# V loaded head by head, folds in halves, end scores apart: one stretch of an attention and MoE kernel

## The chip, the core and the metric

The kernel runs on one core of one Trainium2 chip. The metric is the device time of one execution in microseconds (us); the number for a kernel is the median of its runs. The engines are TensorE (PE; PEld is its weight load), VectorE (DVE), ScalarE (ACT), GpSimd (POOL) and SyncE (SP). DMAs are issued by POOL, which also converts float32 to bfloat16 on the way, by SP, and at the start by ACT.

## The reference, cut

```python
# q, k, v: (8 batches, 8 heads, 576 positions, 64), float32
scores = q @ k.transpose(0, 1, 3, 2) / 8
mask = (rel >= 0) & (rel < 64)          # rel = query position - key position
attn = softmax(where(mask, scores, -1e9))
x = (attn @ v).transpose(0, 2, 1, 3).reshape(4608, 512)
h = x @ w_in                            # 512 -> 2048
out = (h * clip(h + 3, 0, 6) / 6) @ w_out   # 2048 -> 512
```

Causal attention with a window of 64 positions feeds a two-layer network with a hard-swish between the layers.

## The kernel before

The work has two halves that are woven into each other. The network runs over nine tiles of 512 tokens: for tile t the first products (`s1_part`, L737) give 16 blocks of hidden units, each finished by one ACT and one DVE instruction (L750, L755), and the second products (`s2_part`, L776) give four blocks of 128 output rows, 16 matmuls each, which are copied (L789) and stored by SP. Attention of batch t + 1 is placed inside tile t.

Attention of a batch works on pairs of heads, 0 to 3 (`NG` = 4). For batches 0 and 1, q and k arrive with nine positions per partition (tiles `Aq`, `Ak`) and PE turns them ("folds") into `Fq` and `Fk`. In batch 1 `fold_four` (L540) does that for two pairs at once: 36 transposes for q and 36 for k into two PSUM tiles of two banks each, then one copy of 128x1152 per tile (L545), q on ACT and k on DVE here. From batch 2 on, q and k arrive by rows (`nq`, `nk`) and SP issues two DMA transposes into `Tq` and `Tk` (L391), each after the loads that it reads.

`scores` (L581) multiplies q by k for a group of items in one PE piece: an item is a pair, or "e", the last 64 queries of all pairs. Each item has a PSUM tile of its own, an exponential on ACT (L597) and a masking on DVE (L606). In batch 1 the groups are (0, 1) and ("e", 2, 3). `pv_rows` (L626) multiplies by V for a pair, DVE normalises (L636, L637), `turn_x` (L652) transposes the result into `xT` (copy at L368); "e" goes through `pv` (L678, ACT L684 and L687, DVE L698).

V lies in one tile, `V`, by blocks of 128 positions and by pairs. Four blocks are loaded; seven more, each half a block further on, are made by copies between partition halves (`shift_v`, L456), four blocks and three blocks in separate copies. In batch 1 there is a shift for each pair, which the planner gives to POOL, ACT or DVE. Batch 1's V comes by `load_vrows` (L389): four loads with 128 positions of all eight heads each, and a fifth, `load_vrows(1, NE)` for the end rows. Batch 0 has also used `load_vhead`, one load with all four blocks of one head.

What stands where is decided before the program is written. Each operation is put down with its reads and writes, an estimate of its duration, a stream and a priority, and `Plan.solve` places one after the other on the engine and the PSUM tile that let it start first. PSUM has three kinds of tile: "n" (`pn`, two of one bank), "b" (`pb`, one of two banks) and "a" (`pa`, two of two banks). Landing times of DMAs are fixed by hand for the first loads: `LANDED` and, for the loads on POOL after them, the list `NEXT`. POOL's loads and its `hold` operations form one chain through `then`, in the order in which they are put down; its other work is placed between them. The result is one fixed order for each engine. `hold` (L854) is a small POOL copy that keeps the next batch's loads behind a DMA transpose.

Of the kernel before, what the change touches and what calls it, by code (L numbers as in the profile page):

```python
# [11 lines left out]
BF16 = mybir.dt.bfloat16  # L12
# [12 lines left out]
    "POOL": (4600, 6820, 7920, 9640, 10900, 11600, 11950, 12350, 12800, 13200),  # L25
    "ACT": (3200,),
}
NEXT = (15140, 16470, 19010, 21590, 24580, 26640, 29180, 30650, 32050, 32490, 35020, 37600, 39010, 40440, 41280, 42170, 43000, 43830, 44270, 45500, 46500, 47500, 48500, 49500, 50500, 51500, 52500, 53300, 54000)
MARGIN = 300
COLD_PE = 6500  # L30
FAR = 8.0e9
# [191 lines left out]
def kernel(  # L223
# [9 lines left out]
    nc = tc.nc  # L233
    P = nc.NUM_PARTITIONS
    B, H, S, D = q.shape
# [33 lines left out]
    def bank(op, name):  # L269
        s, k = op.got[name]  # L270
        return banks[k][s][:] if k == "n" else banks[k][s][:, 0, :]
# [15 lines left out]
    def t_key(n, b, g):  # L287
        return ("T" if b >= ROWS_FROM else "F") + n, g

    def home(b, g, h):  # L290
        return 1 - h if 0 < b < ROWS_FROM and g % 2 else h
# [61 lines left out]
    def act(n):  # L353
        return 160 + n / 1.2

    def dve(n, fast=1):
        return 150 + n / 0.96 / fast
# [4 lines left out]
    def cpy(eng):  # L362
        return {"DVE": nc.vector.tensor_copy, "ACT": nc.scalar.copy, "POOL": nc.gpsimd.tensor_copy}[eng]
# [9 lines left out]
    def pe(dur, em, reads, writes, stream, alloc=None, kinds=("n",), after=(), mode="f"):  # L373
        op = add("PE", dur, em, reads=reads, writes=writes, stream=stream, after=after)
        op.alloc, op.kinds, op.mode = alloc, kinds, mode
        return op
# [61 lines left out]
    def load_vhead(b, g, h, after=()):  # L438
        return dma(NE * P, 16, V[:, 0:NE, g, 2 * h * D : 2 * h * D + D], v[b, 2 * g + h, 0:MAIN, :].rearrange("(k s) d -> s k d", k=NE),
                   writes=[("V", g, 0, blk) for blk in (2 * h, 2 * h + 1)], eng="POOL", after=after)  # L440
# [85 lines left out]
    def fold_four(g0, b, gate, kinds=("b", "a")):  # L526
# [24 lines left out]
            e.frees = (x,)  # L551
        return op

    def scores(b, items, gate, stream="att", pr=300, masked=False, kinds=("a",)):

        names = tuple(("S", b, x) for x in items)
        keys = [("ps", n) for n in names]
        ends = [x == "e" for x in items]
        gs = sorted({g for x in items for g in (range(NG) if x == "e" else (x,))})
        if masked:  # L560
            add_far = pe(2 * mm(MAIN) + 50, None, ["far", "ident"], keys, stream, alloc=names, kinds=kinds, after=gate)

            def far_em():
                for h in range(2):
                    nc.tensor.matmul(wide(add_far, names[0])[:, h, :], lhsT=ident[:], rhs=far[:].rearrange("p j c -> p (j c)"),
                                     start=True, stop=False)

            add_far.emit = far_em
        op = pe(sum(2 * (NG if e else NM) * 14 for e in ends) + (100 if masked else 0), None,
                [t_key(n, b, g) for g in gs for n in "qk"], keys,  # L570
                stream, alloc=None if masked else names, kinds=kinds, after=gate, mode="r")

        def em():
            for x, name in zip(items, names):
                to = wide(add_far if masked else op, name)
                for y in range(NG if x == "e" else NM):
                    g, j = (y, NM) if x == "e" else (x, y)
                    for h in range(2):
                        r = slice(home(b, g, h) * D, (home(b, g, h) + 1) * D)
                        for o, w in k_cols(b, r, g, j):  # L580
                            nc.tensor.matmul(to[o, home(b, g, h) if x == "e" else h, y * D : (y + 1) * D], lhsT=w,  # L581
                                             rhs=q_cols(b, r, g, j), start=not masked,
                                             stop=not masked or y == NM - 1)

        op.emit = em
        got = []
        for x, name, key in zip(items, names, keys):
            if x == "e":
                n, w, p_, m0 = NG, ("p9", b % 2), p9[b % 2], 1
            else:  # L590
                i = npt[0] % NPT
                npt[0] += 1
                n, w, p_, m0 = NM, ("pT", i), pT[i], 0
                got.append(i)

            def ex(name=name, n=n, p_=p_):
                nc.scalar.activation(out=p_[:].rearrange("p j h c -> p h j c"),  # L597
                                     in_=wide(add_far if masked else op, name)[:, :, 0 : n * D].rearrange("p h (j c) -> p h j c", c=D),
                                     func=EXP, scale=scale)

            e = add("ACT", act(n * P), ex, reads=[key], writes=[w], prio=pr)
            e.frees = (name,)
            if not masked:
                def mk(n=n, p_=p_, m0=m0):
                    pp = p_[:].rearrange("p j h c -> p (j h c)")
                    nc.vector.tensor_tensor(out=pp, in0=pp, in1=mask[:, m0 : m0 + n, :, :].rearrange("p j h c -> p (j h c)"), op=MULT)  # L606

                add("DVE", dve(n * P, 2), mk, reads=["mask"], writes=[w], port=True, prio=pr + 100)
        return op, got
# [184 lines left out]

    def attend(b, first, second, stream="att", rows=()):
        a, i0 = scores(b, (0, 1), first, stream)
        z, i1 = scores(b, ("e", 2, 3), second + (a,), stream, kinds=("b", "a"))
        todo = list(zip((0, 1, "e", 2, 3), (*i0, None, *i1)))
        if rows:
            todo.append(todo.pop(2))  # L800
        for x, i in todo:
            if x in rows:
                _, *og = pv_rows(b, x, i, (z,), stream)
                turn_x(b, x, *og, stream, kinds=("b", "a"))
            else:
                pv(b, x, i, (z,), stream)
# [16 lines left out]
    def load_v(b, blks):  # L823
        for blk in blks:
            then(load_vrows(b, blk, chain))
# [20 lines left out]
    def then(op):  # L846
        chain[0] = op
        return op
# [62 lines left out]
        then(add("POOL", pool(NG * P), lambda n=n: nc.gpsimd.memset(by_block(n, N_)[D:P, KB - 1, :, :], 0.0),  # L911
             writes=[("n" + n, NE, 0), ("n" + n, NE, 1)], after=chain))
    then(add("POOL", 1900, lambda: nc.gpsimd.memset(V[:, :, :, D + 2 : 2 * D], 1.0), writes=["V2"], after=chain))
    load_v(1, range(NE))

    for t in range(NTT):
        head = HEAD if len(x_parts(t)[1]) == 1 else 0
        if t == 0:
            head = HEAD0
            for gs, n in ((range(2), head), (range(2, NG - 1), SOON)):  # L920
                for fc in range(n):
                    s1_part(t, fc, gs)
        else:
            for fc in range(head):
                s1_part(t, fc, range(NG - 1))

        def seen(t, fc, head):
            return 0 if fc >= head else 2 if t == 0 and fc >= SOON else NG - 1

        hs = [s1_finish(t, fc, s1_part(t, fc, range(seen(t, fc, head), NG))) for fc in range(NFC)]  # L930
        ys = {}
        us = range(4 * t, 4 * t + 4)
        if t == 0:
            for pair in (us[:2], us[2:]):
                for part in (range(0, NFC // 2), range(NFC // 2, 3 * NFC // 4), range(3 * NFC // 4, NFC)):
                    for u in pair:
                        ys[u] = s2_part(u, part)
                for u in pair:
                    s2_close(u, ys[u][-1])
        else:  # L940
            for u in us:
                for cols in (((0, DM),) if u < NT // P - 1 else ((0, 3 * P), (3 * P, DM))):
                    s2_close(u, s2_part(u, range(NFC), cols=cols)[-1], cols)
        b = t + 1
        if b < B:
            if b == 1:
                gate = (hs[4],)
                cast_v(iv, 0, 2, (THREE,) * 3, parts=REST, prio=-2500, pieces=(1,))
                scores(0, ("e",), gate, "pick", kinds=("b", "a"))
                pv(0, "e", None, (), "pick")  # L950
                then(load_vrows(1, NE, chain))
                for g in range(0, NG, 2):
                    fold_four(g, 1, gate)
                for g in range(NG):
                    shift_v(g, g + 1, THREE)
                attend(1, gate, gate, "pick", ROWS)
            else:
                for g in range(0, NG, 2):
                    shift_v(g, g + 2, ("ACT", "DVE") if b == 2 else ("DVE",))
                attend(b, (hs[LATE if b > ROWS_FROM else -1],), (hs[-1],))  # L960
            if b + 1 < B:
                load_rows(b + 1)
# [53 lines left out]
```

## Time and profile before

| | us |
|---|---|
| median of 3 runs | 300.29 (299.33 to 302.04) |
| the profiled execution | 299.94 |
| its span, first to last instruction | 298.2 |
| PE busy in the span | 287.2 (96%) |
| ACT busy | 206.5 (69%) |
| DVE busy | 199.8 (67%) |
| POOL busy | 121.9 (41%) |
| mean granted TensorE clock | 0.999 |

Times in the profile are us from the first instruction. A row of the instructions in order of time has the start, the length, the engine, the line, the operation, what it writes and reads, how many there are, and in brackets how long the engine sat idle before and what ended that. In DMA rows the last number is the median time from issue to landing in us. Matmuls are pipelined, so the length of one row reaches into the next one's start. Busy shares are averages over stages with different limits.

### The profile page before, as it was taken

The numbers are of one execution on the slowest core, as the hardware profiler recorded it, in microseconds if no ns is written. First come the engines' busy times: TensorE is split into PE (matmuls) and PEld (weight loads), VectorE is DVE, ScalarE is ACT, GpSimd is POOL, SyncE is SP. The second block draws the span as 40 slices with busy tenths as digits, with TensorE's granted clock in tenths as the row PEclk, the third lists the DMA queues.
The fourth block names the chain that finished last, engine by engine and source line by source line (L and its number), as shares of the span: only waits on it lengthen the run. The fifth ranks groups of instructions, "written<-read, shape, count | busy, mean of one in ns | idle before, by whom it ended". The sixth has DMA issues, their size and how long they took to land.

```text
span 298.2 us, 6926 instructions
## 1 busy us (share of the span) xinstructions
PE 287.2 (96%) x2780; PEld 153.4 (51%) x2825; DVE 199.8 (67%) x327; ACT 206.5 (69%) x319; POOL 121.9 (41%) x170
## 2 busy tenths in 40 slices
PE   6899998999999999999999999999999999999996
PEld 6544555445544554455687554455445544444443
DVE  4768639777777975878678767878677868106700
ACT  3878636887968795778687958886787768227611
POOL 8884667069547916930992069405000000000000
PEclk9999999999999999999999999999999999999999
DMA  8999999999999999989996899969900110110011
GB/s 187 189 207 206 203 191 176 191 95 151 132 201 150 117 151 196 169 55 209 142 165 40 139 184 171 68 118 167 116 2 35 37 70 1 37 70 35 0 73 70
DMA packets 137680, 36.66 MB, mean 123 GB/s; under 512 B 126256, under 2 KB 132912, under 8 KB 137648
## 3 DMA queue, kind: packets, MB, share of 16 engines
q0 software_dynamic: 98816, 17.80, 73.9%
q1 hardware_dynamic: 38688, 18.12, 25.2%
q8 instruction: 22, 0.36, 0.5%
q10 hardware_dynamic: 144, 0.29, 0.4%
q14 instruction: 10, 0.08, 0.1%
HBM read 36.70 MB, written 9.44 MB: 155 GB/s over the span
## 4 chain that ended last, share of the span: by engine, by line
PE 81%; DMA 10%; POOL 3%; issue 3%; DVE 2%; ACT 0%; POOLq 0%; DVEq 0%
PE pn L776 36%; PE pn L737 16%; PE pa L737 12%; PE pb L737 9%; DMA Aq<-in_q_dram 4%; DMA V<-in_v_dram 4%; PE pa L678 4%; DMA Ak<-in_k_dram 2%; PE pa L581 2%; PE pa L776 1%; PE pb L678 1%; DVE opg L637 1%; DVE pT L606 1%; POOL V L389 0%; POOL Aq L389 0%
## 5 line engine op out<-in xcount | busy, mean ns | idle before, releaser
L776 PE MATMUL pn<-wout,gT 128*128 128x512 bf16 x533 | 124.9, 379 | 2.1 <-issue 1.1
L737 PEld LDWEIGHTS <-win 128*128 128x128 bf16 x640 | 62.0, 98 | 60.5
L776 PEld LDWEIGHTS <-gT 128*128 128x128 bf16 x592 | 54.5, 98 | 58.0 <-issue 0.2
L737 PE MATMUL pn<-xT,win 128*128 128x512 bf16 (+1 forms) x270 | 61.1, 357 | 0.3
L750 ACT ACTIVATE t<-pn,half 128x512 bf16<-128x512 f32 x62 | 42.6, 689 | 8.7 <-PE pn L737 8.3
L755 DVE SCALAR_TENSOR_TENSOR gT<-t,pa 128x512 bf16<-128x512 bf16 x47 | 32.2, 687 | 24.2 <-ACT t L750 23.9
L737 PE MATMUL pa<-xT,win 128*128 128x512 bf16 (+1 forms) x202 | 48.0, 358 | 0.4
L755 DVE SCALAR_TENSOR_TENSOR gT<-t,pn 128x512 bf16<-128x512 bf16 x62 | 42.5, 686 | 8.4 <-ACT t L750 8.1
L389 POOL DMA_DIRECT2D nk<-in_k_dram x55 | 42.0, 797 | 4.8 <-DMA Tk<-nk 4.1
L389 POOL DMA_DIRECT2D V<-in_v_dram x40 | 33.2, 848 | 14.4 <-PE pa L678 12.0
L750 ACT ACTIVATE t<-pa,half 128x512 bf16<-128x512 f32 x47 | 32.2, 686 | 8.9 <-PE pa L737 8.5
L698 DVE TENSOR_TENSOR xT<-pa,rec 64x512 bf16<-64x512 f32 (+1 forms) x48 | 32.0, 667 | 9.3 <-ACT rec L687 8.4
L737 PE MATMUL pb<-xT,win 128*128 128x512 bf16 (+1 forms) x153 | 36.3, 357 | 0.5 <-issue 0.5
L755 DVE SCALAR_TENSOR_TENSOR gT<-t,pb 128x512 bf16<-128x512 bf16 x35 | 24.0, 686 | 16.2 <-ACT t L750 16.1
L789 ACT COPY osb<-pn 128x512 f32<-128x512 f32 x18 | 10.5, 585 | 33.1 <-PE pn L776 33.1
L684 ACT ACTIVATE rec<-pa 64x512 f32<-64x512 f32 (+1 forms) x48 | 27.6, 574 | 5.1 <-PE pa L678 4.0
L750 ACT ACTIVATE t<-pb,half 128x512 bf16<-128x512 f32 x35 | 24.2, 690 | 7.6 <-PE pb L737 7.5
L389 POOL DMA_DIRECT2D nq<-in_q_dram x30 | 27.0, 900 | 3.2 <-DMA wout<-in_moe_w_out_dram 1.6
L597 ACT ACTIVATE pT<-pa 128x1024 bf16<-128x1024 f32 x25 | 24.6, 1021 | 1.0 <-PE pa L581 0.9
L606 DVE TENSOR_TENSOR pT<-pT,mask 128x1024 bf16<-128x1024 bf16 x28 | 19.2, 704 | 3.7 <-ACT pT L597 3.6
L678 PEld LDWEIGHTS <-V 128*128 128x128 bf16 x448 | 16.8, 98 | 6.7 <-DVE xT L698 0.8
L854 POOL COPY scrap<-Tq 128x1 bf16<-128x1 bf16 x5 | 0.9, 189 | 45.3 <-DMA Tq<-nq 45.3
(93 smaller groups left out, 203.9 us busy)
## 6 DMA issues: line engine op xcount, KB each, us to landing
out_dram<-osb SPq DMA_DIRECT2D x35, 256.0 KB, 3.1
V<-in_v_dram POOLq DMA_DIRECT2D x28, 128.0 KB, 5.7
nq<-in_q_dram POOLq DMA_DIRECT2D x24, 128.0 KB, 4.7
nk<-in_k_dram POOLq DMA_DIRECT2D x41, 64.0 KB, 4.0
wout<-in_moe_w_out_dram POOLq DMA_DIRECT2D x4, 512.0 KB, 14.5
win<-in_moe_w_in_dram POOLq DMA_DIRECT2D x3, 512.0 KB, 9.3
V<-in_v_dram POOLq DMA_DIRECT2D x12, 64.0 KB, 6.0
Aq<-in_q_dram POOLq DMA_DIRECT2D x2, 288.0 KB, 13.7
```

The source lines that it names most:

```text
L389: em = lambda: e.dma_start(out=out_ap, in_=in_ap)
L581: nc.tensor.matmul(to[o, home(b, g, h) if x == "e" else h, y * D : (y + 1) * D], lhsT=w, rhs=q_cols(b, r, g, j), start=not masked, stop=no ...
L597: nc.scalar.activation(out=p_[:].rearrange("p j h c -> p h j c"), in_=wide(add_far if masked else op, name)[:, :, 0 : n * D].rearrange("p ...
L606: nc.vector.tensor_tensor(out=pp, in0=pp, in1=mask[:, m0 : m0 + n, :, :].rearrange("p j h c -> p (j h c)"), op=MULT)
L678: nc.tensor.matmul(wide(op, name)[:, h, y * D : (y + 1) * D], lhsT=V[:, blk, g, h * D : h * D + P], rhs=p_[:, y, home(b, g, h) if end else ...
L684: add("ACT", act(n), lambda h=h: nc.scalar.activation(out=rc[rows[h], 0:n], in_=wide(op, name)[rows[1 - h], h, 0:n], func=LN), reads=[key] ...
L698: nc.vector.tensor_tensor(out=o, in0=a, in1=z, op=MULT)
L737: nc.tensor.matmul(bank(op, name)[:, to : to + n], lhsT=win16[:, g, fc * P : (fc + 1) * P], rhs=xT[:, g, o : o + n], start=(g == 0), stop= ...
L750: nc.scalar.activation(out=t1[ti][:], in_=bank(op, name), func=RELU, bias=half[:], scale=1.0 / 6.0)
L755: nc.vector.scalar_tensor_tensor(out=gT[:, fc, :], in0=t1[ti][:], scalar=1.0, in1=bank(op, name), op0=MIN, op1=MULT)
L776: nc.tensor.matmul(bank(op, name)[:, 0:n], lhsT=gT[:, fc, col : col + P], rhs=wout16[:, fc, js], start=(fc == 0), stop=(fc == NFC - 1))
L789: alts = {e: (f(n), (lambda e=e: cpy(e)(out=osb[oi][:, js], in_=bank(op, name)[:, 0:n])), False) for e, f in (("DVE", dve), ("ACT", act))}
```

## The change

Batch 1's V is loaded head by head: eight loads of 64 KB in the place of four of 128 KB, and the fifth load of the end rows as before. Pairs 2 and 3 of batch 1 are folded by a new function, first q and then k as two operations, each with two PSUM tiles of which one bank is used, and with one copy of 128x576 for each pair. Pairs 0 and 1 stay with `fold_four`. In batch 1 the scores of "e" become a group of their own, put down after (2, 3). In `NEXT` four fixed landing times are replaced by eight between the same neighbours.

```diff
-NEXT = (15140, ..., 39010, 40440, 41280, 42170, 43000, 43830, 44270, 45500, ...)
+NEXT = (15140, ..., 39010, 40440, 40863, 41287, 41711, 42135, 42558, 42982, 43406, 43830, 44270, 45500, ...)
...
+    def fold_two(n, g0, b, gate, kinds=("b", "a")):
+
+        pair = (g0, g0 + 1)
+        names = tuple(("F", n, b, g) for g in pair)
+        op = pe(R * 38 + 30, None, [("A", n, g) for g in pair] + ["fold"], [("ps", x) for x in names], "pick",
+                alloc=names, kinds=kinds, after=gate, mode="r")
+
+        def em():
+            for j in range(R):
+                for g, x in zip(pair, names):
+                    to = bank(op, x).bitcast(BF16)
+                    for h in range(2):
+                        r, o = (slice(y * D, (y + 1) * D) for y in (h, home(b, g, h)))
+                        nc.tensor.transpose(out=to[o, j * D : (j + 1) * D], in_=A[n][r, g, j, :], identity=fold[r, :])
+
+        op.emit = em
+
+        def ev(eng, g, x):
+            cpy(eng)(out=F_[n][:, g, :].rearrange("d (p j) -> d p j", j=R),
+                     in_=bank(op, x).bitcast(BF16)[:, 0:S].rearrange("d (j p) -> d p j", p=D))
+
+        for g, x in zip(pair, names):
+            alts = {e: (c, (lambda e=e, g=g, x=x: ev(e, g, x)), False) for e, c in (("DVE", dve(S)), ("ACT", act(S) - 30))}
+            e = add("DVE", 0, None, reads=[("ps", x)], writes=[t_key(n, b, g)], alts=alts, stream="copy", prio=300)
+            e.frees = (x,)
+        return op
...
     def attend(b, first, second, stream="att", rows=()):
         a, i0 = scores(b, (0, 1), first, stream)
-        z, i1 = scores(b, ("e", 2, 3), second + (a,), stream, kinds=("b", "a"))
+        if rows:
+            z, i1 = scores(b, (2, 3), second + (a,), stream, kinds=("b", "a"))
+            z, _ = scores(b, ("e",), (z,), stream, kinds=("b", "a"))
+            i1 = (None, *i1)[1:]
+        else:
+            z, i1 = scores(b, ("e", 2, 3), second + (a,), stream, kinds=("b", "a"))
...
-    load_v(1, range(NE))
+    for g in range(NG):
+        for h in range(2):
+            then(load_vhead(1, g, h, chain))
...
                 for g in range(0, NG, 2):
-                    fold_four(g, 1, gate)
+                    if g == 0:
+                        fold_four(g, 1, gate)
+                    else:
+                        for n in "qk":
+                            fold_two(n, g, 1, gate)
```

The planner's order changes with it, and only in this stretch to speak of. On PE the q fold of pairs 2 and 3 comes after 16 instead of 24 second products behind the first scores; then four products, the k fold, four products, the scores of pairs 2, 3 and "e", eight products, and the first product with V. On POOL the order is: heads 1 to 8, the end rows of V, a shift of pair 0, a q and a k load of batch 2, a shift of pair 3, a q load, the second shift of pair 3, and the other seven loads of batch 2; before, seven of these loads came ahead of all four of POOL's shifts. On ACT one shift of pair 1 stands ahead of the exponentials of pairs 2, 3 and "e", in that order; before, one shift of pair 3 stood ahead of "e", 2 and 3. On DVE four shifts stand ahead of the masking of pairs 2 and 3 and "e". In batch 2 four more second products come ahead of the first product with V.

More of the change, by code (lines that the diff above doesn't have):

```diff
@@ L27 @@
 }
-NEXT = (15140, 16470, 19010, 21590, 24580, 26640, 29180, 30650, 32050, 32490, 35020, 37600, 39010, 40440, 41280, 42170, 43000, 43830, 44270, 45500, 46500, 47500, 48500, 49500, 50500, 51500, 52500, 53300, 54000)
+NEXT = (15140, 16470, 19010, 21590, 24580, 26640, 29180, 30650, 32050, 32490, 35020, 37600, 39010, 40440, 40863, 41287, 41711, 42135, 42558, 42982, 43406, 43830, 44270, 45500, 46500, 47500, 48500, 49500, 50500, 51500, 52500, 53300, 54000)
 MARGIN = 300
```

## The prediction

> **What bounds the kernel now.** I read the head of the profile's page first, then the busy time by stretches, then the instructions in order of time in the stretch that the change touches.
>
> ```profile
> span 298.2 us, 6926 instructions
> PE 287.2 (96%) x2780; PEld 153.4 (51%) x2825; DVE 199.8 (67%) x327; ACT 206.5 (69%) x319; POOL 121.9 (41%) x170
> ...
> 32.40:52.10 19.70, 18.40 (x364) 10.34 (x369) 12.29 (x21) 11.80 (x17) 13.43 (x18) 1.00 1.87 189
> 52.10:66.10 14.00, 13.89 (x77) 6.26 (x78) 10.89 (x19) 11.26 (x18) 3.55 (x5) 1.00 0.88 144
> ```
>
> In a row of stretches the first pair after the length is TensorE (PE). It is the bound: 287.2 of 298.2 us. The whole change lies between 32.4 and 52.1 us, where PE does batch 1's attention between the second matrix products of token tile 0. There it is busy 18.40 of 19.70 us, so 1.30 us is all that a better order can give back. In the next 14.00 us it misses 0.11: once tile 1's first products begin, a gain or a loss made before them goes straight to the end. These are the steps of the touched stretch:
>
> ```profile
> 35.86 5.39 PE L776 MATMUL pn<-wout,gT 128*128 128x512 bf16 x23
> 41.17 0.48 PE L540 MATMUL pb<-fold,Aq 64*64 64x64 bf16 x36
> 41.48 0.50 PE L540 MATMUL pa<-fold,Ak 64*64 64x64 bf16 x36
> 41.91 1.90 PE L776 MATMUL pn<-wout,gT 128*128 128x512 bf16 x7
> 43.74 0.29 PE L581 MATMUL pa<-Fq,Fk 64*128 64x64 bf16 x8
> ...
> 44.43 0.82 PE L776 MATMUL pn<-wout,gT 128*128 128x512 bf16 x3
> ...
> 45.71 0.45 PE L626 MATMUL pa<-V,pT 128*64 128x65 bf16 x16 [0.45 <-ACT p L597]
> ...
> 48.22 0.45 PE L626 MATMUL pa<-V,pT 128*64 128x65 bf16 x16 [0.34 <-DVE pT L606]
> 48.83 0.81 PE L776 MATMUL pn<-wout,gT 128*128 128x512 bf16 x3 [0.16 <-issue]
> ...
> 51.65 0.40 PE L652 MATMUL pb<-ident,opg 128*128 128x128 bf16 x4 [0.19 <-DVE opg L637]
> ...
> 52.12 1.68 PE L737 MATMUL pn<-xT,win 128*128 128x512 bf16 x7
> ```
>
> The bracketed waits are 0.45, 0.34, 0.16 and 0.19, together 1.14 us. What stands behind them is V: the chain of waits has one DMA piece, and ScalarE (ACT) sits behind it.
>
> ```profile
> 33.45 10.97 DMA V<-in_v_dram
> 44.53 0.51 ACT L456 COPY V<-V 64x384 bf16<-64x384 bf16 x1 [1.69 <-DMA V<-in_v_dram]
> 45.06 0.60 ACT L597 ACTIVATE p<-pa 128x512 bf16<-128x512 f32 x1
> 45.55 1.02 ACT L597 ACTIVATE pT<-pb 128x1024 bf16<-128x1024 f32 x1
> ...
> 46.51 0.19 DVE L636 RECIPROCAL rsum<-pa 128x8 f32<-128x8 f32 x1
> 46.74 0.69 DVE L637 TENSOR_TENSOR opg<-pa,rsum 128x512 bf16<-128x512 f32 x1
> ```
>
> The fourth V load lands at 33.45 + 10.97 = 44.42, because each load carries rows of all heads and the first shift needs all four. ACT has the shift ahead of three exponentials, and only these set the score banks free. The DVE rows are one normalisation, 0.9 with its steps.
>
> **The change, part by part.**
>
> *V head by head.* Four loads of 128 KB become eight of 64 KB: the same bytes and packets. Their issue and their landing have these rows (the last four lines, with us to landing at the end, are the issues at 24.64, 27.17, 32.59 and 41.38 us):
>
> ```profile
> 5.94 3.00 POOL L389 DMA_DIRECT2D V<-in_v_dram  x4
> ...
> 32.59 1.75 POOL L389 DMA_DIRECT2D V<-in_v_dram  x2 [0.16 <-issue]
> 35.55 0.69 POOL L389 DMA_DIRECT2D V<-in_v_dram  x1 [1.22 <-DMA wout<-in_moe_w_out_dram]
> ...
> 41.38 0.89 POOL L389 DMA_DIRECT2D nq<-in_q_dram  x1 [1.22 <-DMA Ak<-in_k_dram]
> ...
> Aq<-in_q_dram POOLq DMA_DIRECT2D x1, 288.0 KB, 14.4
> Ak<-in_k_dram POOLq DMA_DIRECT2D x1, 288.0 KB, 13.3
> V<-in_v_dram POOLq DMA_DIRECT2D x1, 128.0 KB, 10.4
> nq<-in_q_dram POOLq DMA_DIRECT2D x1, 128.0 KB, 6.9
> ```
>
> The first row is batch 0's head loads: 0.75 us each, against 0.88 for a load by rows, so the issues cost 8 x 0.75 - 4 x 0.88 = 2.5 us more on GpSimd (POOL). The bracketed waits show a limit of eight: the fifth load of this run, at 35.55, waits for the landing of the load eight places before it, and so on to the eighth, at 41.38. Now heads 5 to 8 stand in these four places: head 8 is issued at 41.38 at the latest, when k of pairs 2 and 3 has landed (27.17 + 13.3 = 40.47 by the DMA row; 41.38 by the POOL row).
>
> When does it land? The load of q at 41.38 took 6.9 us with V loads 2 to 4 (1,024 packets each), the last V rows (512), a q and a k load (1,024 each) and itself in the queue: 6,656 packets. Head 8 has heads 2 to 8 there, 512 each, 3,584: 6.9 x 3584 / 6656 = 3.7, so 45.1. The bounds are 3.4 us (below) and the 10.97 of V before. The earlier heads come at the pace of before: the third V load landed at 32.59 + 10.4 = 43.0, three loads after 40.47, so 0.84 for two heads: head 2 by 41.3, head 4 by 42.15, head 6 by 43.0.
>
> *The queue that it is moved past.* Batch 2's q and k loads, and three shift copies of V on POOL, stand behind those eight issues, and the order puts pair 3's shift, which waits for head 8, ahead of eight of the ten loads. Rows of the tail, and what hangs on it:
>
> ```profile
> 45.81 2.72 POOL L456 COPY V<-V 64x384 bf16<-64x384 bf16 x4
> ...
> 49.35 0.70 POOL L389 DMA_DIRECT2D nq<-in_q_dram  x1
> ...
> 53.17 3.00 SPq L391 DMA_TRANSPOSE Tq<-nq  x1
> ...
> 62.21 0.19 POOL L854 COPY scrap<-Tk 128x1 bf16<-128x1 bf16 x1 [11.47 <-DMA Tk<-nk]
> ...
> 66.02 0.71 PE L581 MATMUL pa<-Tq,Tk 64*64 64x64 bf16 x64
> ```
>
> From 41.38: head 8 0.75, last V rows 0.69, shift 0.68, q 0.88, k 0.88 (45.26, head 8 landed), pair 3's shift 0.68, q 0.89, shift 0.68, five loads at 0.89: the last q issue at 51.96, against 49.35. That is 2.6 us late. SyncE's queue starts the transpose of q when the last q load is in, so k's transpose shifts as much: landed about 62.2 + 2.6 = 64.8. Batch 2's first scores come at 66.02. So 1.2 us of cover is left; once it is gone every further microsecond on POOL is one of PE's. Next behind the same landing are batch 2's V loads:
>
> ```profile
> V<-in_v_dram POOLq DMA_DIRECT2D x1, 128.0 KB, 3.4
> ...
> 73.67 0.63 PE L678 MATMUL pb<-pT,V 128*128 128x64 bf16 x16
> ```
>
> The first row is the one issued at 62.74. The last of the five lands by about 62.74 + 4 x 0.88 + 3.4 = 69.7 now and 72.3 then; the products that use them start at 73.67, with four more second products ahead of them in the new order. Hidden, with room for a shift of V.
>
> *Folds in halves, scores apart.* The number of transposes is the same. Copies of 128x576 replace half as many of 128x1152; the small ones have these rows from batch 0:
>
> ```profile
> L518 ACT COPY Fk<-pn x2: 645/645/645, 6.3 to 10.7; 128x576 bf16<-128x576 bf16 x2
> L518 DVE COPY Fk<-pa x1: 758/758/758, 7.9 to 7.9; 128x576 bf16<-128x576 bf16 x1
> ```
>
> In the new order the q fold comes after 16 instead of 24 products: (41.17 - 35.86) / 24 = 0.221 each, so 35.86 + 3.54 = 39.40; q landed at 24.64 + 14.4 = 39.04. Half a fold takes 0.31, four products 0.88: 40.59. There the k fold wants the k load: 40.47 or 41.38 as above. I take 40.59, because the DMA row gives the landing itself; the other costs 0.8 there. Then 0.43, four products, 41.90; the k copies are done at 41.02 + 0.76 = 41.78, just hidden. Scores 0.69 to 42.59, eight products to 44.36.
>
> *ACT.* Its shift now needs only heads 3 and 4 (42.15): 42.2 to 42.7, exponentials to 43.7, 44.8 and 45.4, about 2 us earlier than before. The first product with V at 44.36 waits for nothing, the second for its bank until 44.9 (0.15), then two pieces of four products and the third bring PE to 47.43. VectorE (DVE) masks the last group at 45.4 to 46.2 and normalises at 0.9 each: 47.1, 48.0, 48.9. The second turn waits 0.2 to 0.3. Pair 3's product comes at about 50.15, POOL's two shifts for it being done at 47.5. Tile 1 starts at about 51.8 instead of 52.12.
>
> *The sum.* -0.3 us. Best: all four waits go, -1.14. Worst without a further stall: k late, +0.8, of which the remaining waits absorb about 0.4, and up to 0.7 for a normalisation or exponential that comes one place later: +0.8. The profiled execution took 299.94 (span 298.2 and 1.74 around it), 0.35 under the median of 300.29. Forecast 299.6.
>
> *A rule against the change.* DVE's V copies now fall between POOL's issues instead of after them. One such copy did run over an issue before: DVE at 44.55 and the q load at 44.86, which took 0.91 against 0.90 for the one before it.
>
> ```profile
> 44.55 1.26 DVE L456 COPY V<-V 64x512 bf16<-64x512 bf16 x3 [1.15 <-DMA V<-in_v_dram]
> ...
> 44.86 0.91 POOL L389 DMA_DIRECT2D nq<-in_q_dram  x1
> ```
>
> The Trainium skill (SBUF — State Buffer, "Who interferes with whom") says that a VectorE copy in a two-port mode holds the port pair that GpSimd needs to write descriptors, and that the later one blocks fully. By the row POOL loses 0.01 us; by that rule it loses the whole length of each copy, and the trace does not agree.
>
> **The rivals.**
> - *Nothing gained* (A): the k fold waits till 41.38 and ACT's shift, now ahead of pair 2's exponential, costs the rest. For it: the POOL row. Against: the DMA row. 299.94 + 0.5 = 300.4.
> - *All waits go* (C): 299.94 - 1.14 = 298.8. Against it: pair 1's product wants a bank behind two exponentials.
> - *Held issues* (L): each of four V copies on DVE, 1.26 / 3 us, holds POOL for its whole length: 1.7 us later, against a cover of 1.2 less the gain of 0.3: 299.6 + 0.8 = 300.4. Against it the row of 0.91. This is what the rule of the Trainium skill above would make of it.
> - *Slower* (B): head 8 lands late. It holds POOL's shift of pair 3, hence PE's fourth product with V and the q and k loads. It decides from a landing of about 46.2 on, when the cover of Tk is used, and stalls the product itself from 50.15 - 2.25 = 47.9. At 50.3 the product is 2.4 late and Tk, at 64.8 + 5.0, meets scores at 65.7 + 2.4: 1.7 more. 299.6 + 4.1 = 303.7. At the 10.97 of before (52.35): 4.45 and 1.75, 305.8. For it: the fourth V load took 10.97 from issue to landing. Against: it waited behind q, k and weights, which head 8 does not.
>
> **How the numbers follow.** Forecast 0.38, A 0.20, C 0.07, L 0.03, B 0.22; 0.10 is left for what no row shows, 0.06 of it on the slow side. One per cent, 3 us, is about what a measurement of this kernel can tell from no change. Only half of B (0.11) and the 0.06 lie beyond it: slower 0.17; faster 0.04, since the stretch holds 1.30 us; same 0.79. The likeliest case with A and C runs from 298.2 (298.8 and the 0.6 between the profiled execution and the fastest of the three runs, 299.33) to 300.7; B's middle carries the range to 303.8.
>
> **What would show it.** Right: the copy of V on ACT starts near 42.2, no wait over 0.3 us before a product with V, the last q issue near 52.0, Tk's scrap copy near 64.8, batch 2's scores at 65.7 with no DMA ahead of them. Wrong: PE waiting for Ak at the k fold (A), for POOL at pair 3's product or for Tk ahead of batch 2's scores (B), or POOL issues over 1 us beside DVE copies (L).

## The result, and the profile after

| | before | after |
|---|---|---|
| median, us | 300.2 (299.33 to 302.04, 6 runs) | 303.25 (302.4 to 303.46, 6 runs) |
| ratio, 95% interval | 1 | 1.0098 [1.0079, 1.0118] |
| profiled execution, us | 299.94 | 303.13 |
| its span | 298.2 | 301.4 |

The kernel after is 2.9 (by the ratio) to 3.05 us (by the medians) slower, 0.98 to 1.02 per cent. The prediction had forecast 299.6, a little faster; the time lies inside its range, but it moved the other way, as far as the 1 per cent bound beyond which "slower" had a chance of 0.17. The head of the page and the stretches of the profile after:

```profile
span 301.4 us, 6990 instructions
...
32.40:52.10 19.70, 19.63 (x373) 10.38 (x372) 13.44 (x24) 12.10 (x20) 13.17 (x18) 1.00 1.46 160
52.10:66.10 14.00, 14.00 (x68) 6.21 (x65) 10.71 (x18) 10.92 (x17) 1.99 (x3) 1.00 1.25 169
66.10:86.30 20.20, 17.92 (x281) 9.54 (x281) 11.64 (x19) 15.52 (x24) 15.84 (x21) 1.00 1.48 119
```

and the last of these stretches in the kernel before:

```profile
66.10:86.30 20.20, 19.88 (x289) 10.64 (x294) 14.35 (x23) 16.32 (x26) 12.50 (x18) 1.00 1.60 153
```

The stretch that the change touches is now full: TensorE (PE) is busy 19.63 of 19.70 us, where it was 18.40. Part of that is a later start of this execution (last section): e11, with the same order there and a start as early as before, is busy 18.90. The loss is in a stretch that the change does not touch: between 66.1 and 86.3 us, batch 2's attention, PE misses 2.28 us (before, in the same window, 0.32). The instructions of PE in order of time, kernel after:

```profile
52.14 0.81 PE L764 MATMUL pn<-xT,win 128*128 128x512 bf16 x3
...
66.97 0.71 PE L608 MATMUL pa<-Tq,Tk 64*64 64x64 bf16 x64 [0.85 <-DMA Tk<-nk]
...
75.44 0.22 PE L705 MATMUL pb<-pT,V 128*128 128x64 bf16 x2
76.56 0.58 PE L705 MATMUL pb<-pT,V 128*128 128x64 bf16 x14 [0.90 <-ACT V L456]
...
81.82 0.64 PE L705 MATMUL pb<-pT,V 128*128 128x64 bf16 x16 [0.53 <-DVE xT L725]
...
86.33 0.81 PE L764 MATMUL pa<-xT,win 128*128 128x512 bf16 x3
...
88.12 0.38 PE L764 MATMUL pa<-xT,win 128*128 128x512 bf16 x1 [0.33 <-DVE xT L725]
...
99.00 0.64 PE L608 MATMUL pa<-Tq,Tk 64*128 64x64 bf16 x32
```

and the start of tile 2 and the scores of batch 3 in the kernel before:

```profile
83.68 0.81 PE L737 MATMUL pa<-xT,win 128*128 128x512 bf16 x3
...
95.86 0.64 PE L581 MATMUL pa<-Tq,Tk 64*128 64x64 bf16 x32
```

Tile 1 starts at 52.14, where it started before (52.12). Then four waits come that were not there: batch 2's scores for Tk, the first product with V for a shift of V on ScalarE (ACT), a product for the normalised `xT`, and one more for `xT` at tile 2's start. Between the same milestones of the two kernels: tile 1's start to the scores 14.83 against 13.90 us (+0.93); the scores to tile 2's start 19.36 against 17.66 (+1.70; the two brackets show 1.43 of it, since a bracket begins only at the modelled end of the instruction ahead); tile 2's start to batch 3's scores 12.67 against 12.18 (+0.49). These make 3.12 of the 3.2 us between the spans.

The chain of waits says where they come from; its lines are start, length and what the end waited on:

```profile
41.36 4.27 DMA V<-in_v_dram
...
45.75 0.64 POOL V L456
46.39 0.58 issue
46.97 0.89 POOL nq L389
...
47.90 0.50 POOL V L456
48.40 0.82 POOL nk L389
...
52.67 5.27 DMA nq<-in_q_dram
...
58.00 3.03 SPq L391
...
61.13 0.52 SPq L389
...
61.87 5.05 DMA Tk<-nk
...
70.26 1.54 POOL V L389 x2
71.80 3.61 DMA nq<-in_q_dram
...
76.53 0.83 ACT V L456
```

Head 8 of V lands, GpSimd (POOL) makes pair 3's shift between its loads for batch 2, the last q load goes out at 52.67, SyncE's queue transposes q, stores, transposes k, and only then come POOL's V loads for batch 2 and ACT's shift of that V. (The piece at 71.80 carries the name of the load beside which the last V load lands that the shift needs; the piece at 76.53 is the second of ACT's two shifts.) In the chain of the kernel before, nothing but PE's own work stands from 51.65 us on to tile 2, apart from 0.4 us of issue.

### The profile page after: what moved, and what is told of

The parts are those of the page before. It is cut to its first block, busy times and chain, and to the rows that moved or that the text cites. A ratio compares the mean times of both kernels' runs of the same rounds, so it can differ in the third digit from the quotient of the medians.

```text
span 301.4 us, 6990 instructions
## 1 busy us (share of the span) xinstructions
PE 293.1 (97%) x2825; PEld 154.2 (51%) x2825; DVE 199.2 (66%) x328; ACT 207.1 (69%) x321; POOL 123.1 (41%) x173
## 4 chain that ended last, share of the span: by engine, by line
PE 79%; DMA 7%; POOL 3%; issue 3%; DVE 2%; ACT 2%; SPq 1%; POOLq 0%; DVEq 0%; ACTq 0%
PE pn L803 33%; PE pn L764 15%; PE pa L764 12%; PE pb L764 9%; PE pa L705 3%; DMA nq<-in_q_dram 3%; PE pa L608 2%; DMA Tk<-nk 2%; DVE xT L725 2%; DMA V<-in_v_dram 1%; DMA stage<-in_q_dram 1%; PE pa L803 1%; POOL V L389 1%; SPq L391 1%; POOL nq L389 1%
## 5 line engine op out<-in xcount | busy, mean ns | idle before, releaser
L803 PE MATMUL pn<-wout,gT 128*128 128x512 bf16 x560 | 129.3, 379 | 0.0
L782 DVE SCALAR_TENSOR_TENSOR gT<-t,pn 128x512 bf16<-128x512 bf16 x61 | 41.8, 686 | 9.1 <-ACT t L777 8.9
L389 POOL DMA_DIRECT2D V<-in_v_dram x44 | 35.6, 830 | 19.3 <-PE pa L705 12.2
L764 PE MATMUL pb<-xT,win 128*128 128x512 bf16 (+1 forms) x160 | 38.2, 358 | 0.0
L782 DVE SCALAR_TENSOR_TENSOR gT<-t,pb 128x512 bf16<-128x512 bf16 x36 | 24.7, 686 | 16.3 <-ACT t L777 16.3
L624 ACT ACTIVATE pT<-pa 128x1024 bf16<-128x1024 f32 x26 | 25.6, 1021 | 2.4 <-PE pa L608 2.2
```

Source lines behind the costliest of these rows:

```text
L389: em = lambda: e.dma_start(out=out_ap, in_=in_ap)
L764: nc.tensor.matmul(bank(op, name)[:, to : to + n], lhsT=win16[:, g, fc * P : (fc + 1) * P], rhs=xT[:, g, o : o + n], start=(g == 0), stop= ...
L782: nc.vector.scalar_tensor_tensor(out=gT[:, fc, :], in0=t1[ti][:], scalar=1.0, in1=bank(op, name), op0=MIN, op1=MULT)
L803: nc.tensor.matmul(bank(op, name)[:, 0:n], lhsT=gT[:, fc, col : col + P], rhs=wout16[:, fc, js], start=(fc == 0), stop=(fc == NFC - 1))
```

## The experiments

Each row below is one profile. "Tk" is the time of the scrap copy that follows Tk's landing, counted from the start of tile 1, so that a later or earlier start of an execution drops out. The waits are PE's, for Tk, for a shift of batch 2's V, and for `xT` inside batch 2. Each ratio is against runs of the kernel before on the same chip, whose median lay between 299.9 and 300.2; differences between two experiments are given by the ratios first.

| kernel | Tk after tile 1's start | waits: Tk, V, xT | median, us | ratio, 95% interval |
|---|---|---|---|---|
| before | 10.09 | 0, 0, 0 | 300.2 | 1 |
| e1_heads | 12.17 | 0, 0.45, 0 | 300.78 | 1.0029 [1.0017, 1.0042] |
| e2_folds_scores | 9.58 | 0, 0, 0 | 300.49 | 1.0019 [1.0009, 1.0029] |
| e4_noshiftpool | 10.93 | 0, 0, 0 | 299.73 | 0.9998 [0.9984, 1.0012] |
| e5_delay | 11.76 | 0, 0, 0 | 300.54 | 1.0021 [1.0011, 1.003] |
| e7_pair3 | 12.74 | 0, 0, 0 | 300.64 | 1.0022 [1.0001, 1.0042] |
| e12_store | 13.48 | 0, 0.94, 0.53 | 301.5 | 1.0047 [1.0032, 1.0062] |
| e10_middelay | 13.98 | 0, 0.88, 0.53 | 302.52 | 1.0075 [1.0057, 1.0092] |
| e6_longdelay | 14.59 | 0.60, 0.85, 0.53 | 302.98 | 1.0092 [1.0062, 1.0122] |
| after | 14.91 | 0.85, 0.90, 0.53 | 303.25 | 1.0098 [1.0079, 1.0118] |
| e11_earlyv | 15.95 | 2.17, 0, 0 | 302.68 | 1.0074 [1.0055, 1.0093] |

The theory: nothing in the touched stretch costs time; the loss is the lateness of batch 2's last q and k loads, carried on to Tk, to V and to `xT`. The rivals: one part of the change costs it by itself; the copies on POOL do, whatever the time of Tk; the new order of batch 2 does.

**e1_heads: the head loads alone**

```diff
-    load_v(1, range(NE))
+    for g in range(NG):
+        for h in range(2):
+            then(load_vhead(1, g, h, chain))
```

(on the kernel before, with the eight landing times in `NEXT`.)

> The kernel before with one part of the change: V of batch 1 head by head, with the eight fixed landing times. Theory T (the loss comes from batch 2's q and k loads, issued late behind the eight V loads, so that k's transpose Tk and batch 2's V come late): last q load issued near 52 instead of 49.35, scrap copy of Tk near 65 to 67 instead of 62.2, PE waiting for Tk or for batch 2's V; 302 to 303.5. Rival F (the loss comes from the halved folds and the new order of scores, or of the second products of tile 1): 300.2 plus or minus 0.5. Rival S (0.84 us of the loss is lost before 31 us and belongs to the start of the execution, not to the change): the second products start at 30.7 or at 31.5, not tied to this part.

Measured 300.78, by the ratio +0.9: theory T's 302 to 303.5 missed, and just over F's range. Here the planner gives POOL one shift, behind the first q load of batch 2; the last q issue is at 50.48 and Tk 12.17 after tile 1's start. The one new wait is 0.45 us before the first product with V of batch 2, for a shift on DVE.

**e2_folds_scores: folds in halves and scores apart, V by rows**

```diff
-    for g in range(NG):
-        for h in range(2):
-            then(load_vhead(1, g, h, chain))
+    load_v(1, range(NE))
```

(on the kernel after, with the old `NEXT`.)

> The changed kernel with V of batch 1 loaded by rows again, so only the folds in halves and the scores of the end queries apart. T: the stretch gains up to 1.1 us (the four waits), last q load at 49.4 and Tk as before, no wait for Tk; 299.0 to 299.9. F: 302 or more, with V loaded as before. S: start of the second products at 30.7 or 31.5 here too.

Measured 300.49, by the ratio +0.6, where T had 299.0 to 299.9. Tk comes no later, as T had it, but in the touched stretch a wait of 0.42 for a normalised row is left (at 51.84). The wait of 0.33 for `xT` at tile 2 is there and the other three of the kernel after are not. So neither part makes the loss alone, and their sum, +1.5, is half of it.

**e4_noshiftpool: everything, but no shift of batch 1's V on POOL**

```diff
-                    shift_v(g, g + 1, THREE)
+                    shift_v(g, g + 1, ("ACT", "DVE"))
```

> The changed kernel with the shifts of V of batch 1 allowed on ScalarE and VectorE only, so that nothing on GpSimd waits for head 8 ahead of batch 2's loads. T, if the shift of pair 3 on GpSimd is the main hold: last q load issued 1.5 to 2.5 us earlier than 52.67, Tk 2 us earlier, 301 to 302. T, if the eight issues and the limit of eight loads in flight are the main hold: last q load near 51.5 to 52, time 302.5 to 303. F: 303.2, as the changed kernel.

Measured 299.73, under every time that was expected: the whole loss is gone, 3.0 us by the ratios and 3.5 by the medians. The rows of e4 that answer to the chain:

```profile
49.55 0.77 POOL L389 DMA_DIRECT2D nq<-in_q_dram  x1
...
63.03 0.19 POOL L886 COPY scrap<-Tk 128x1 bf16<-128x1 bf16 x1 [12.03 <-DMA Tk<-nk]
...
85.40 0.38 PE L764 MATMUL pa<-xT,win 128*128 128x512 bf16 x1 [0.33 <-DVE xT L725]
```

The last q issue is 3.1 us earlier than in the kernel after, Tk 4.0, and of the four waits the 0.33 is left. That the shifts on POOL are needed for the loss is shown; by what they act, not yet.

**e5_delay: lateness without heads or more shifts**

```diff
+                if b == ROWS_FROM and kb == NE and n == "q":
+                    then(add("POOL", 100, lambda: nc.gpsimd.memset(idle[:], 0.0), writes=["idle"], after=chain))
```

(on e2, ahead of the last q and k loads; a memset of 128x5400.)

> The kernel of e2_folds_scores with one GpSimd memset of a scratch tile, some 4.8 us, ahead of the last q and k loads of batch 2; the order on every other engine is that of e2_folds_scores. T: last q load near 54, scrap copy of Tk 66 to 67, PE waits near 1 us for Tk and again for batch 2's V; 2 to 3.5 us slower than e2_folds_scores, so 301.5 to 303. F: as e2_folds_scores within 0.5 us.

The expectation missed: 300.54, as e2. The memset moved the last q issue by 5.0 us (53.19 against 48.21) but Tk by only 2.6 (64.26 against 61.66): with the queue run empty meanwhile, the transpose of q began 2.7 us after that issue instead of 5.0. Tk at 11.76 after tile 1's start is free.

**e6_longdelay and e10_middelay: the same, longer**

```diff
-  lambda: nc.gpsimd.memset(idle[:], 0.0)
+  lambda: (nc.gpsimd.memset(idle[:], 0.0), nc.gpsimd.memset(idle[:, 0:3300], 0.0))   # e10: 0:2360
```

> V by rows as before, folds in halves, scores apart, and two GpSimd memsets (about 4.6 and 2.8 us, 7.4 together) ahead of the last q and k loads of batch 2; nothing else of the kernel after. Theory T (the loss is nothing but the lateness of batch 2's last q and k loads: Tk past the start of its scores, then batch 2's V behind it): Tk's scrap copy near 67.0, against 64.3 with the short memset; PE waits about 0.9 us for Tk, then about 0.9 for a V shift and 0.5 for xT; 2.5 to 3 us over the kernel with folds and scores alone (300.49), so 303 to 303.5. Rival R (it is the head loads or GpSimd's shifts themselves, whatever the time of Tk): as with folds and scores alone, 300.5 within 0.5, although Tk is late. Between the two (301 to 302): Tk costs its own wait alone and the rest is of another kind.

> The kernel with folds and scores alone and the two GpSimd memsets, the second shorter: about 6.7 us together instead of 7.5. Tk's scrap copy then comes 13.8 us after tile 1's first products (14.6 with 7.5 us, 11.8 with 4.6). From the two rows of the longer delay (PE waited 0.60 for Tk and 0.85 for a V shift on ACT) batch 2's V begins to be late when Tk is later than 14.59 - 0.60 - 0.85 = 13.1 us after tile 1's start, and Tk itself only from 14.0. Theory T1 (the V chain decides first): no wait for Tk, a wait of 0.5 to 0.8 for the V shift, a smaller one for xT, and 0.7 to 1.5 over the kernel with the short memset (300.54): 301.2 to 302.0. Rival (the loss begins with PE's wait for Tk): 300.3 to 300.8, no wait over 0.4 between 66 and 86 us.

POOL's row and PE's waits in e6:

```profile
48.72 7.51 POOL L846 MEMSET idle<- 128x5400 bf16 x2
...
67.14 0.71 PE L608 MATMUL pa<-Tq,Tk 64*64 64x64 bf16 x64 [0.60 <-DMA Tk<-nk]
...
76.69 0.58 PE L705 MATMUL pb<-pT,V 128*128 128x64 bf16 x14 [0.85 <-ACT V L456]
81.95 0.64 PE L705 MATMUL pb<-pT,V 128*128 128x64 bf16 x16 [0.53 <-DVE xT L725]
```

And in e10:

```profile
48.56 6.72 POOL L846 MEMSET idle<- 128x5400 bf16 x2
...
75.95 0.58 PE L705 MATMUL pb<-pT,V 128*128 128x64 bf16 x14 [0.88 <-ACT V L456]
81.21 0.64 PE L705 MATMUL pb<-pT,V 128*128 128x64 bf16 x16 [0.53 <-DVE xT L725]
```

e6 is 302.98: a kernel with V by rows and nothing but a late pair of loads shows the waits of the kernel after, and is 2.2 to 2.5 us over e2. That is the theory, and no rival is left that needs the heads or the copies themselves. (The 0.33 at tile 2 stands in e2 already, and has another cause; see the next section.) e10 tells which wait comes first. Tk is just in time there (scores at 66.38, no wait), and 1.6 to 2.0 us over e5 are lost all the same, more than the 0.7 to 1.5 expected, since Tk came 13.98 and not 13.8 after tile 1's start. The 0.88 for V is what the limit of 13.1 in the expectation gives for that (13.98 - 13.1). So in this order batch 2's V is late as soon as Tk comes within 0.9 us of the time from which it would be late itself.

**e11_earlyv: batch 2's V loads ahead of the copy that waits for Tk**

```diff
 order of POOL:
   last q, last k
-  scrap copy (waits for Tk)
   five V loads of batch 2
+  scrap copy (waits for Tk)
```

> The kernel after, with the five V loads of batch 2 issued on GpSimd right behind its last k load, ahead of the small copy that waits for Tk; every other engine's order is that of the kernel after. Theory T1 (of the 3.2 us, the chain Tk, V loads, V shift, product holds 1.7): Tk still lands about 67, or later by what five more loads in the queue cost the transposes; PE's wait for Tk 0.9 or more stays, the waits of 0.90 for the V shift and 0.53 for xT go; 301.2 to 301.8. Rival (those waits come from the order of batch 2 in the kernel after, not from the loads' time): they stay, 303. Mishap to look for: V loads and transposes collide and Tk comes over 1 us later, 302 to 303 with a longer wait for Tk.

302.68. The two waits of batch 2 are gone, as the theory had it; the mishap came too:

```profile
57.27 4.43 SPq L391 DMA_TRANSPOSE Tq<-nq  x1
61.80 0.52 SPq L389 DMA_DIRECT2D out_dram<-osb  x1
62.54 3.64 SPq L391 DMA_TRANSPOSE Tk<-nk  x1
...
67.68 0.71 PE L608 MATMUL pa<-Tq,Tk 64*64 64x64 bf16 x64 [2.17 <-DMA Tk<-nk]
68.32 4.45 PE L803 MATMUL pn<-wout,gT 128*128 128x512 bf16 x11
```

Beside the V loads the issue of q's transpose takes 4.43 us instead of 3.03, and Tk comes 1.0 later still (15.95). The profiled execution took 303.77 and lost another 1.7 us in the last row quoted (4.45 where the kernel after has 2.76; see the last section); the other three took 302.19 to 302.75.

**e7_pair3: POOL may shift pair 0 but not pair 3**

```diff
-                    shift_v(g, g + 1, THREE)
+                    shift_v(g, g + 1, THREE if g < NG - 1 else ("ACT", "DVE"))
```

> The kernel after, but pair 3's shift of V in batch 1 may go to ACT or DVE only; GpSimd keeps pair 0's shift, ahead of batch 2's loads. Theory T (what counts is what stands among GpSimd's issues of batch 2's q and k: two copies and a wait for head 8): last q issue near 50.5, Tk's scrap copy near 64, no wait of PE for Tk, time 299.7 to 300.4. Rival (any V copy on GpSimd in this stretch, by port or queue): 301 to 302.

300.64, 0.2 over the expected range and below the rival's. POOL still copies pair 0's shift, ahead of its q and k loads, and waits for no head; Tk is 12.74 after tile 1's start, and there is no wait for Tk or V in batch 2; the 0.33 at tile 2 is left. What counts is what stands among the loads.

**e12_store: a store out of the way of the last loads**

```diff
 order of SP:
-  third store of tile 0
   transpose to Tq, store, transpose to Tk
+  third store of tile 0
```

> The kernel after, with one store of SyncE's queue (the third of tile 0, issued near 50.8 us while the last six q and k loads of batch 2 are on their way) put behind Tk's transpose; every other engine's order is that of the kernel after. It asks where the last q load's 5.3 us from issue to landing come from (3.6 before). Theory S (the store takes the queue's time: in the kernel after two loads land 1.8 and 2.2 us behind the one ahead of them instead of 0.87): last q load lands 3.6 to 4.2 us after its issue, Tk 13.4 to 13.8 us after tile 1's start instead of 14.9, no wait for Tk, a smaller wait for the V shift (0.3 to 0.6); 301.5 to 302.5. Rival (the loads stand too close together after a late start, and drain no faster): landing 5 or more, Tk as before this edit, 303.0 to 303.5.

301.5, by the ratios 1.5 us below the kernel after (1.75 by the medians), with POOL's order as there. DMA issues at the last q load, kernel after (us to landing last):

```profile
nq<-in_q_dram POOLq DMA_DIRECT2D x1, 64.0 KB, 5.3
```

and e12, with its time of Tk:

```profile
nq<-in_q_dram POOLq DMA_DIRECT2D x1, 64.0 KB, 3.9
...
65.81 0.19 POOL L886 COPY scrap<-Tk 128x1 bf16<-128x1 bf16 x1 [11.52 <-DMA Tk<-nk]
```

Without the store of 256 KB, issued at 51.02 among the last loads, the last q load lands 1.4 us sooner after its issue. These are single profiles, and in e11, where the store stands as in the kernel after (issued at 50.41), that load took 4.5: by these the store's price is anything from 0.6 to 1.4. The wait for Tk is gone; the wait for V is 0.94, more than the 0.3 to 0.6 expected and than the limit of 13.1 gives for a Tk at 13.48. From Tk's copy to the first shift of V it took 8.7 us here (65.81 to 74.54), 8.4 in the kernel after and 7.5 in e7, so that limit moves with V's loads; whether the moved store, now issued beside them, is what slows them is not shown. The profiled execution, at 302.21, is the slowest of the six.

**e8_folds_heads and e9_scores_heads: e4 with one part less**

```diff
 e8:  z, i1 = scores(b, ("e", 2, 3), second + (a,), stream, kinds=("b", "a"))   # one group again
 e9:  fold_four(g, 1, gate)                                                     # for all pairs
```

> The kernel after without GpSimd's shifts in batch 1 (ACT and DVE only) and with the scores of the end rows in one group with pairs 2 and 3 as before: heads and folds in halves remain. In its order 32 second products of batch 2's tile stand ahead of the first product with V and 12 behind the last one, as in the kernel after. Theory T: a wait of 0.3 for xT near 85.4, time 299.7 to 300.0. Rival (scores apart give what little gain there is): 300.3 or more.

> The kernel after without GpSimd's shifts in batch 1 (ACT and DVE only) and with pairs 2 and 3 folded four tiles at once as before: heads and scores apart remain. Batch 2's order has 28 second products ahead of the first product with V and 16 behind, as in the kernel before. Theory T: no wait for xT near 85, time 299.2 to 299.6, the best of these. Rival (folds in halves are what takes the waits out of the stretch from 32 to 52): waits of 0.3 to 0.8 there, 299.9 to 300.4.

e8 took 300.29, ratio 0.9997 [0.9978, 1.0016], between the two expectations: undecided. e9 took 300.55, 1.0026 [1.0003, 1.0049], and missed: waits of 0.32 and 0.55 us stand in the touched stretch where e4 has none, so by these profiles it is the folds in halves, with the planner's order that comes with them, that take waits out there (e4 starts later, but e11, with folds in halves and a start as early as e9's, has no wait over 0.19 there), while the 0.33 at tile 2 is gone as expected. No version here is faster than the kernel before by more than its interval.

## Why the prediction was wrong, by its own steps

The step that failed is the lateness of Tk, 2.6 us in the sum and 4.8 measured, and behind it "hidden, with room for a shift of V". That the time lies inside the range is luck: rival B carried the range up to 303.8, for a late head 8 that did not come. Nor is one per cent what a measurement here can tell from no change: the interval of the result is 0.2 per cent to either side.

*Bound, folds, scores, ACT: right.* In the profile after, the second products of tile 0 begin at 31.49, 0.84 later than in that of before (30.65), which the change does not cause: e11, with the same order on each engine that far, starts them at 30.66 (last section). With 0.84 added, the q fold is due at 40.24 and stands at 40.24, ACT's shift at 43.0 (42.81), pair 3's product at 51.0 (50.42), tile 1 at 52.6 (52.14). In e11, whose order is that of the kernel after up to there and which starts at 30.66, tile 1 starts at 51.74; "about 51.8" was forecast. No wait over 0.3 us stands ahead of batch 1's products with V. So up to tile 1 the gain of 0.3 was there, in e11's profile; no kernel here turned it into a shorter time.

*Head 8: nearly right.* It landed at 45.63 (45.1 forecast), ahead of B's 46.2. But POOL waited for it even so:

```profile
45.75 0.64 POOL L456 COPY V<-V 64x512 bf16<-64x512 bf16 x1 [0.61 <-DMA V<-in_v_dram]
46.97 0.89 POOL L389 DMA_DIRECT2D nq<-in_q_dram  x1 [0.58 <-issue]
...
52.67 0.73 POOL L389 DMA_DIRECT2D nq<-in_q_dram  x1
```

*The tail of POOL: the step that failed.* "The last q issue at 51.96", 2.6 us late, was 52.67, 3.3 late: 0.61 of waiting for head 8 and 0.58 of idle time behind the shift (POOL's other two shifts have none behind them; what it is stays open) were not in the sum, and other terms were a little long. "So k's transpose shifts as much" was worse: the landing of the last q load was taken as unchanged at 3.6 us and was 5.3. A landing is not an issue plus a constant. The last q loads of the kernel before and of e2, issued at 49.35 and 48.21:

```profile
nq<-in_q_dram POOLq DMA_DIRECT2D x1, 64.0 KB, 3.6
```

```profile
nq<-in_q_dram POOLq DMA_DIRECT2D x1, 64.0 KB, 4.8
```

Issued 1.14 us apart, they land together at 53.0, behind a k load that lands at 52.6 and 52.5: the load comes when those ahead of it are in. In the kernel after, the last seven loads were issued 0.87 apart with the store among them, and by e11 and e12 the store has 0.6 to 1.4 of the 1.7; the rest is not told apart. 3.3 + 1.7 = 5.0 us, by the rows of q's transpose 58.00 - 53.17 = 4.8: Tk at 67.05 instead of 64.8.

*"Hidden, with room for a shift of V": wrong.* The limit of 1.2 us of cover was that of Tk. V's is tighter. From Tk's scrap copy at 67.05 to the product at 76.56 are 9.5 us: 0.6 to the first V issue, 4.2 for the five, landed by 75.4 (the four that the shift reads), and then the first of ACT's two shifts, 0.95. The prediction had 0.5 + 4 x 0.88 + 3.4 = 7.4 to the landing, where it was 8.4, since the loads landed 3.5 to 5.1 us after their issue and not all in the 3.4 of the first; and it set no duration for the shift. By e6 and e10 the V chain is late from Tk at 13.1 us after tile 1's start, Tk itself from 14.0; in e1, with four second products fewer ahead of the first product with V, V is late by 0.45 at 12.17 already. In the forecast Tk would have come at 64.8 - 51.8 = 13.0: just free. So the mis-sized lateness decided, 4.8 for 2.6, and the missing V chain turned it into more than PE's wait for Tk: of the 3.2 us, 0.93 is Tk, 1.70 V with the `xT` behind it, and 0.49 batch 2's order.

*Batch 2's order* was read only for what it puts ahead of the first product with V (four more second products, 0.8 us of cover for V). The same four are missing behind the last one, 12 instead of 16, and PE waits 0.33 for `xT` at tile 2. It shows in every profile with 12 behind it, e2, e4, e5 and e8 among them, and not in e1 and e9, which keep 16. From tile 2's start to batch 3's scores e2, e4 and e8 take the 12.67 us of the kernel after, e1 and e9 12.18 and 12.19.

*The rivals.* A did not come. C's waits went in the profile after, beside its later start, but in e11 0.16, 0.16 and 0.19 are left, and C's time did not come. L did not come either: four V copies on DVE ran across the issues of two loads, which took 0.88 each:

```profile
43.45 1.74 DVE L456 COPY V<-V 64x384 bf16<-64x384 bf16 x4
```

```profile
43.39 0.88 POOL L389 DMA_DIRECT2D nq<-in_q_dram  x1
44.26 0.88 POOL L389 DMA_DIRECT2D nk<-in_k_dram  x1
```

The rule of the Trainium skill that is named in the prediction (SBUF — State Buffer, "Who interferes with whom") would have shown as longer issues; the trace does not show them. Whether these copies run in a two-port mode is not seen in it. B had the right chain, head 8, shift on POOL, q and k loads, Tk, at a price of 4.1 us, but made it hang on a head 8 later than 46.2. Head 8 came before that; the queue behind it was late all the same. Of the signs that the prediction listed, the first two held (ACT's shift, no wait before batch 1's products), and the last three failed (last q issue, Tk, scores without a DMA wait).

## What to carry to other kernels

When a step is put into a queue, follow the lateness of the last item in the queue through everything that is chained to it, each link with its own duration and its own cover: the link with the least cover may be behind the one that looks next. A landing time read from one profile is not a constant to be added to another issue time: it holds the wait for the loads that are in the queue. A copy that any of three engines could make is not free on the one that also issues the next stage's loads: taking its three copies off it was worth 3.0 to 3.5 us here, with the rest of the change left as it was.

## What the runs showed of the hardware

*The clock after a wait.* In e11's profiled execution PE waited 2.17 us for Tk, and 1 us behind the wait the granted clock fell. Its stretches around the wait (PEclk is the third column from the right):

```profile
67.50:68.30 0.80, 0.62 (x64) 0.60 (x64) 0.00 (x0) 0.12 (x1) 0.30 (x2) 1.00 0.00 0
68.30:70.30 2.00, 1.91 (x17) 0.82 (x7) 0.84 (x2) 1.82 (x2) 2.00 (x3) 0.60 0.32 27
70.30:72.30 2.00, 2.00 (x6) 0.71 (x5) 0.55 (x1) 0.00 (x0) 2.00 (x4) 0.54 1.76 112
```

The record of the clock in the trace has 0.5 from 68.71 to 72.12, 3.4 us, which these stretches mix with full clock; eleven recorded products took 4.45 us where twelve took 2.76 in the kernel after (67.61 to 70.37). In the other three executions the mean clock over the kernel was 1.00, against 0.994, so it does not come every time, and behind the waits of 0.85 and 0.90 in the kernel after the products keep their pace (2.76 for twelve, 3.62 for sixteen). That the wait is the cause is not shown: in e7's profile the clock was 0.50 from 10.80 to 14.20 too, with no wait over 1.1 us ahead of it, though PE was busy only 2.23 of the 4 us from 4 to 8. The Trainium skill (TensorE: Matmul & The Clock Gate, "Part 1: The HAM clock gate") states half clock after an idle window of about 3.4 us on a grid of its own. Half clock agrees; the wait seen here was shorter than that window, and the measurement decides.

*The same load lands in 2.4 to 5.3 us.* The last q load of batch 2, 64 KB, landed 2.4 us after its issue behind an emptied queue (e6), and in 3.6 (before), 3.9 (e12), 4.8 (e2) and 5.3 us (after) with other loads ahead of it.

*The start moves with the clock.* Of executions with the same order, the second products of tile 0 begin at about 30.6 in some and 31.5 in others. The first transposes show why, kernel before:

```profile
5.30 0.47 PE L513 MATMUL pn<-fold,Aq 64*64 64x64 bf16 x18 [0.93 <-DVE Aq L368]
```

and after:

```profile
5.29 0.69 PE L513 MATMUL pn<-fold,Aq 64*64 64x64 bf16 x18 [0.70 <-DVE Aq L368]
```

The same 18 transposes take 0.69 instead of 0.47 us, and from 10.8 us on 0.47 in both. The trace's record of the clock begins, at full clock, at 4.0 us in the kernel before and 3.9 in e11 (second products from 30.65 and 30.66), at 9.8 in e5 and 10.3 in e4 (31.53 and 31.62); in e7, with the second drop, they begin at 32.13. The kernel after has no such record. What sets the moment in an execution is not shown. Tile 1 absorbs part of the difference (52.08 in e2, 52.50 in e5); what is left is as large as the gain that the change was forecast to make.
